# Retention and top-2 experts in one kernel: x turned on TensorE, expert 0's slots from a one-hot of their own, the state in 64x64 blocks

## Chip, cores, metric

One core of one Trainium2 chip runs the whole program. The metric is device time in microseconds, the median of several executions.

## What is computed

The reference is a retention layer (linear attention with decay) whose output goes into a layer of eight experts, two of which serve each token:

```
for t in range(S):
    state = gamma[None, :, None, None] * state + np.einsum('bhd,bhe->bhde', k[:, :, t], v[:, :, t])
    y[:, :, t] = scale * np.einsum('bhd,bhde->bhe', q[:, :, t], state)
...
logits = x @ w_gate
noise_scale = np.log1p(np.exp(x @ w_noise))
noisy_logits = logits + noise_scale * noise
top2 = np.argpartition(-noisy_logits, 2, axis=1)[:, :2]
...
        h = np.maximum(x[mask] @ w1[e], 0.0)
        out[mask] += top2_w[mask, k, None] * (h @ w2[e])
```

There are 4 sequences of 768 tokens, 8 heads of 64, so x has 3072 rows of 512; each expert has 1024 hidden columns. All inputs are f32. top2_w are the two weights after a softmax over the two.

## The kernel before

**Retention loop** (lines 629 to 656). The sequences are cut into chunks of 128 tokens, 6 to a sequence (b), 24 in all (j). `qk(j)` makes k times q for the 8 heads (two heads share the array, each in 64 of its rows), and DVE multiplies the result by a mask (`am`). `y_mm(j)` adds the earlier state (q times U, for all but a sequence's first chunk) and am times v in the PSUM tile pY, then updates the state pU by four products of 128 columns of k with 128 of v, two heads at once, of which only the two diagonal 64x64 blocks are wanted (not in a sequence's last chunk). ACT copies those blocks to U and takes the sum of squares of pY. `x_scale` makes a power of two of it on DVE. `x_split` has ACT scale pY into f32 (`xs`) and copy that to an f16 high part, GpSimd subtract it to get an f16 low part, and SP issue two DMAs: a transpose of both parts into `xt` and a write to `xbuf` in HBM. Three chunks later `logits` multiplies xt by the gate weights.

**Routing** of a sequence is done by DVE while the next sequence runs in the loop: `route_a` to `route_c` (logits, noise, top two, their one-hots `oh` and `mb`), `route_d` (the slot of each token and choice among the 56 blocks of 128 slots, 7 to an expert), `route_e` for each of the two choices: a one-hot of the slot's lane (`a`, 6 x 128 columns), one of its block (`ob`, 6 x 56), and `bb`, ob times five numbers of the token (two for its index, three for its gate; 6 x 5 x 56 = 1680 columns). `route_f` multiplies a by bb on PE and adds the product to a table `acc`, from which `slots` takes the token and the gate of every slot, and `rows_of` the row indices `idx`. The dictionary `todo` says in which chunk each step is issued.

**Experts.** `gather` fetches rows of xbuf by idx (GpSimd), `x_t` transposes them by DMA into XE, `mm1` makes 8 units of hidden columns (12 matmuls each, then ACT `hh` and DVE `hl`, the f16 high and low parts), `mm2` one block of 128 output rows (24 matmuls), and `put` adds it to `out` in HBM. Weights are split into f16 high and low parts too (`w_load`, `w_sum`, `w_hi` on ACT, `w_lo` on DVE or `w_lo_pool` on ACT and GpSimd). The first 384 slots of expert 0 are known once two sequences are routed. Behind the loop the 11 units of these 384 slots (8 mm1, 3 mm2) are spread by `early` between the last sequence's routing; then come expert 0's columns from 384 on, the other experts in the order of their load (`ranks`), and a loop for what overflows.

The order on every engine is that in which the program issues instructions (`manual_schedule`); each engine runs its own in that order, and DMAs of SP are issued in order too. PSUM has 8 banks: pA three, pY two, pU, pR and pL one each.

## Time and profile before

| | us |
|---|---|
| median of 3 runs | 730.25 (729.0 to 732.25) |
| profiled execution, span from first to last instruction | 727.5 |
| PE busy in it | 678.9 |
| DVE / ACT / POOL busy | 290.4 / 311.2 / 235.6 |

The three runs give the time; of the profiled execution the span is the time that is known, and it is 2.75 us under the median. PE is TensorE, PEld its loading of weights, DVE VectorE, ACT ScalarE, POOL GpSimd, SP the engine that issues most DMAs. Busy shares say little by themselves, since the retention loop and the experts have different limits; the views by stretch of time tell them apart.

### The profile page before, as it was taken

What the parts mean: (1) busy time and instruction counts of PE and PEld (TensorE: products, weight loads), DVE (VectorE), ACT (ScalarE), POOL (GpSimd) and SP (SyncE); (2) the same over time, 40 slices, a digit from 0 to 9 for tenths busy, and PEclk for the clock granted to TensorE, in tenths of its full rate; (3) what the DMA queues carried; (4) which work ended last, traced back from release to release, by engine and by line L of the source; (5) the groups of instructions that cost most, each with busy time, mean ns of one, the idle gap of its engine ahead of it and who ended that gap; (6) DMA issues with size and microseconds to landing.
All of it is one profiled execution on the core that took longest, in us unless ns stands there. A gap on an engine that the chain in (4) does not pass through costs nothing.

```text
span 727.5 us, 12014 instructions
## 1 busy us (share of the span) xinstructions
PE 678.9 (93%) x4789; PEld 428.2 (59%) x4789; DVE 290.4 (40%) x719; ACT 311.2 (43%) x562; POOL 235.6 (32%) x186
## 2 busy tenths in 40 slices
PE   8998797967989999999999999999999999999991
PEld 6898696965558555465545545554555466446540
DVE  4338669656852762215222421522152234215100
ACT  4655363435214554435444534444344445344110
POOL 4665553542243320441144024304311421240021
PEclk9999796757999999999999999999999999999996
DMA  9999898775658963668367636745673685453132
GB/s 334 239 330 324 276 281 243 220 162 194 226 119 235 232 184 108 115 110 271 40 117 124 240 53 123 195 133 95 119 237 67 118 193 167 71 104 59 14 44 30
DMA packets 116057, 119.09 MB, mean 164 GB/s; under 512 B 82560, under 2 KB 82816, under 8 KB 112416
## 3 DMA queue, kind: packets, MB, share of 16 engines
q1 hardware_dynamic: 104080, 91.25, 45.1%
q0 software_dynamic: 11344, 26.22, 19.5%
q8 instruction: 38, 0.62, 0.4%
q10 hardware_dynamic: 576, 0.84, 0.3%
q14 instruction: 19, 0.16, 0.1%
HBM read 72.67 MB, written 26.21 MB: 136 GB/s over the span
## 4 chain that ended last, share of the span: by engine, by line
PE 65%; DMA 11%; DVE 10%; issue 6%; ACT 3%; POOL 2%; SPq 0%; POOLq 0%; ACTq 0%; DVEq 0%
PE pH L672 10%; PE pH L674 10%; PE pH L673 10%; PE pO L702 8%; PE pO L703 8%; PE pO L704 8%; DMA out<-ot,idx 6%; PE pY L320 2%; DVE am L309 2%; DVE bb L478 2%; DMA xe<-xg 2%; PE pY L316 2%; PE pU L324 1%; DMA xg<-xbuf,idx 1%; PE pA L306 1%
## 5 line engine op out<-in xcount | busy, mean ns | idle before, releaser
L693 POOL DMA_INDIRECT out<-ot,idx x54 | 85.6, 1586 | 350.8 <-ACT ot L688 210.5
L672 PE MATMUL pH<-xe,w1h 128*128 128x384 f16 (+4 forms) x544 | 176.0, 324 | 1.5 <-DMA xe<-xg 1.5
L674 PE MATMUL pH<-xe,w1l 128*128 128x384 f16 (+4 forms) x544 | 176.0, 323 | 0.0
L673 PE MATMUL pH<-xe,w1h 128*128 128x384 f16 (+4 forms) x544 | 176.0, 323 | 0.0
L676 DVE SCALAR_TENSOR_TENSOR hl<-pH,hh 128x384 f16<-128x384 f32 (+4 forms) x136 | 74.6, 549 | 207.9 <-ACT hh L675 207.7
L704 PE MATMUL pO<-w2h,hl 128*128 128x512 f16 x384 | 145.5, 379 | 0.3 <-DVE hl L676 0.3
L703 PE MATMUL pO<-w2l,hh 128*128 128x512 f16 x384 | 145.5, 379 | 0.0
L702 PE MATMUL pO<-w2h,hh 128*128 128x512 f16 x384 | 145.5, 379 | 0.0
L675 ACT ACTIVATE hh<-pH 128x384 f16<-128x384 f32 (+4 forms) x136 | 65.7, 483 | 133.5 <-PE pH L674 133.5
L688 ACT ACTIVATE ot<-pO,gse 128x512 f32<-128x512 f32 (+4 forms) x54 | 37.0, 686 | 174.0 <-PE pO L704 169.5
L197 DVE SCALAR_TENSOR_TENSOR w1l<-wst,wsc,w1h 128x1024 f16<-128x1024 f32 x32 | 41.8, 1312 | 106.8 <-ACT w1h L192 106.8
L673 PEld LDWEIGHTS <-w1h 128*128 128x128 f16 x544 | 53.3, 98 | 34.4 <-issue 2.2
L674 PEld LDWEIGHTS <-w1l 128*128 128x128 f16 x544 | 53.3, 98 | 34.3 <-issue 0.3
L672 PEld LDWEIGHTS <-w1h 128*128 128x128 f16 x544 | 53.9, 99 | 32.7 <-issue 0.3
L175 ACT ACTIVATE junk<-wst 128x1024 bf16<-128x1024 f32 x64 | 67.2, 1049 | 3.5 <-DMA wst<-w 3.2
L591 POOL DMA_INDIRECT xg<-xbuf,idx x54 | 56.9, 1054 | 27.1 <-issue 15.4
L704 PEld LDWEIGHTS <-hl 128*128 128x128 f16 x384 | 37.5, 98 | 46.0 <-DVE hl L676 0.8
L702 PEld LDWEIGHTS <-hh 128*128 128x128 f16 x384 | 38.1, 99 | 44.1
L703 PEld LDWEIGHTS <-hh 128*128 128x128 f16 x384 | 37.5, 98 | 44.2
L320 PE MATMUL pY<-vp,am 128*128 128x64 f32 x384 | 60.6, 293 | 0.0
L320 PEld LDWEIGHTS pY<-vp,am 128*128 128x128 f32 x384 | 58.4, 221 | 0.6 <-issue 0.2
L344 POOL TENSOR_TENSOR x<-xs,x 128x512 f16<-128x512 f32 x23 | 29.2, 1269 | 54.8 <-ACT x L343 26.4
(163 smaller groups left out, 767.2 us busy)
## 6 DMA issues: line engine op xcount, KB each, us to landing
wst<-w SPq DMA_DIRECT2D x28, 1024.0 KB, 7.5
in_q<-qT SPq DMA_DIRECT2D x24, 256.0 KB, 4.6
in_k<-kT SPq DMA_DIRECT2D x24, 256.0 KB, 4.7
in_v<-vt SPq DMA_DIRECT2D x24, 256.0 KB, 4.9
in_kt<-kt SPq DMA_DIRECT2D x24, 256.0 KB, 5.0
xbuf<-x SPq DMA_DIRECT2D x24, 256.0 KB, 3.7
...
```

The costliest lines, as they stand in the source:

```text
L175: nc.scalar.activation(junk, st[:, i * 1024:(i + 1) * 1024], AF.Square, accum_out=ss[:, i:i + 1])
L320: nc.tensor.matmul(pY[:, 2 * i + s, :], AM[j][:, s, i, :], VP[j][:, 2 * i + s, :], start=(not c and i == 0 and s == 0), stop=True, skip_gr ...
L591: nc.gpsimd.indirect_dma_start(out=x[:n], out_offset=None, in_=xbuf[:128 + B0 * S] if e == 0 and t < 3 else xbuf, in_offset=bass.IndirectO ...
L672: nc.tensor.matmul(p[:, :n], whi, xh, start=(k == 0), stop=False)
L673: nc.tensor.matmul(p[:, :n], whi, xl, start=False, stop=False)
L674: nc.tensor.matmul(p[:, :n], wlo, xh, start=False, stop=(k == KT - 1))
L675: nc.scalar.activation(hh[:, f, n0:n1], p[:, :n], AF.Relu)
L676: nc.vector.scalar_tensor_tensor(hl[:, f, n0:n1], p[:, :n], 0.0, hh[:, f, n0:n1], op0=OP.max, op1=OP.subtract)
L693: nc.gpsimd.indirect_dma_start(out=out, out_offset=bass.IndirectOffsetOnAxis(ap=idx[:n, i:i + 1], axis=0), in_=ot[:n], in_offset=None, com ...
L702: nc.tensor.matmul(p, a, WT["2h"][:, f, :], start=(f == 0), stop=False)
L703: nc.tensor.matmul(p, a, WT["2l"][:, f, :], start=False, stop=False)
L704: nc.tensor.matmul(p, c, WT["2h"][:, f, :], start=False, stop=(f == FT - 1))
```

## The change

- **x on TensorE.** x_split makes the f16 high part straight from pY on ACT and the low part on DVE; the DMA transpose and GpSimd's subtraction go. `x_turn` of chunk j - 2 does eight f16 transposes on PE into a new PSUM tile pX (one bank), and ACT copies it to xt. pA has two banks in place of three; mm1 uses pA, pA and pX in turn. logits stands ahead of y_mm and has 12 matmuls of 16 columns in place of 8 of 32 and 16.
- **Routing.** Expert 0's slots have a one-hot of their own over its 7 blocks (`own_a`, `own_b`, `own_c`), in the loop. The other 49 blocks (`rest_c`, `rest_d` on DVE, `rest_e` on PE; 294 and 1470 columns) are made after the loop, in eight parts, four of them ahead of expert 0's columns from 384 on and four between its units; their table is in PSUM (BIGT) until the eleventh unit, then `ranked` sorts it.
- **State.** pU is made by eight products of 64 columns of k with 64 of v, one a head; each writes 64 partitions.
- **Times of other work.** Expert 0's weights are loaded and split some 4 to 9 chunks earlier, the zeros of out are written in chunks 12 to 18, not after the loop, and `early` lets one unit through between smaller steps.

SP's queue around one chunk in the loop before, seven rows (in_q, in_k, in_v and in_kt are the four inputs of a chunk, wst weights, x and xt the two parts of x and their transpose):

```order
L221 DMA in_q<-qT 128x512
L221 DMA in_k<-kT 128x512
L221 DMA in_v<-vt 128x512
L221 DMA in_kt<-kt 128x512
L171 DMA wst_582<-w 128x1024
L346 DMA_TRANSPOSE xt<-x_609 128x8x128
L347 DMA xbuf<-x_609 128x1024
```

and around the thirteenth chunk now (out<-zero is one write of 1 MB):

```order
L353 DMA xbuf<-x_1192 128x1024
L228 DMA in_q<-qT 128x512
L228 DMA in_k<-kT 128x512
L228 DMA in_v<-vt 128x512
L228 DMA in_kt<-kt 128x512
L253 DMA out<-zero 512x1x512
L353 DMA xbuf<-x_1275 128x1024
```

The transposes have left SP's queue, and in some chunks a write of zeros stands there.

DVE in the loop before, where a sequence's route_e stands (L468 to L478) ahead of the next chunk's mask product:

```order
L457 CAST lf<-lb 128x24
L468 TENSOR_TENSOR ob<-blks,lf 128x336
L470 TENSOR_TENSOR a<-lanes,lf 128x768
L478 TENSOR_TENSOR bb<-ob,vv 128x1680
L309 TENSOR_TENSOR am<-pA,ct 128x512 x2
L152 TENSOR_SCALAR p2m<-xss 128x1
L153 TENSOR_SCALAR xsc<-p2m 128x1
```

and now, from the lane one-hot of own_a (L474) over the next chunk's low part of x, mask product and x_scale to own_b:

```order
L474 TENSOR_TENSOR a<-lanes,lf_1269 128x768
L352 SCALAR_TENSOR_TENSOR x_1275<-pY,xsc,x_1275 128x512
L317 TENSOR_TENSOR am<-pA,ct 128x512 x2
L159 TENSOR_SCALAR p2m<-xss 128x1
L160 TENSOR_SCALAR xsc<-p2m 128x1
L162 TENSOR_SCALAR invx<-p2m 128x1
L482 CAST tokb<-gateb 128x6
L483 TENSOR_TENSOR gr<-gateb,tokb 128x6
L484 CAST tokb<-gr 128x6
L485 TENSOR_TENSOR tokb<-gr,tokb 128x6
L495 TENSOR_TENSOR ob_1358<-blks,lf_1269 128x42
L499 TENSOR_TENSOR bb_1360<-ob_1358,tokb 128x210
```

The one-hots of 336 and 1680 columns are gone from here; narrow ones of 42 and 210 are in their place, a chunk later than the lane's, and the low part of x (L352) is new.

DVE where expert 0's columns from 384 on begin, before (L676 is hl of one unit):

```order
L532 TENSOR_REDUCE capd<-cm 128x7
L680 TENSOR_TENSOR i_2484<-wsc_584,wsc_1221 128x1
L683 TENSOR_SCALAR gse<-wacc,i_2484 128x4
L676 SCALAR_TENSOR_TENSOR hl<-pH,hh 128x256 x8
L676 SCALAR_TENSOR_TENSOR hl<-pH,hh 128x192 x8
```

and now (L758 is hl, L541 to L551 one part of rest_c and rest_d):

```order
L485 TENSOR_TENSOR vvb<-gr,vvb 128x12
L758 SCALAR_TENSOR_TENSOR hl<-pH,hh 128x256
L541 TENSOR_TENSOR ob<-blks,lfa 128x294
L543 TENSOR_TENSOR a<-lanes,lfa 128x768
L551 TENSOR_TENSOR bb<-ob,vvb 128x1470
L758 SCALAR_TENSOR_TENSOR hl<-pH,hh 128x256 x2
L541 TENSOR_TENSOR ob<-blks,lfa 128x294
L543 TENSOR_TENSOR a<-lanes,lfa 128x768
L551 TENSOR_TENSOR bb<-ob,vvb 128x1470
```

Between the units' hl there now stand the wide one-hots of the other experts.

The diff, cut to its core:

```diff
-    pU = psum.tile([128, HP, 128], F32, name="pU")
+    pU = psum.tile([128, 512], F32, name="pU")[:, :HP * 64].rearrange("p (a d) -> p a d", a=HP)
...
-        pA = [psum.tile([128, HP, C], F32, name="pA", bufs=3) for _ in range(2)]
+        pA = [psum.tile([128, HP, C], F32, name="pA", bufs=2) for _ in range(2)]
...
         if c < NC - 1:
             for i in range(HP):
-                nc.tensor.matmul(pU[:, i, :], IN["kt", j][:, i * 128:(i + 1) * 128],
-                                 VP[j][:, 2 * i:2 * i + 2, :].rearrange("p h d -> p (h d)"),
-                                 start=(c == 0 and i == 0), stop=True, skip_group_check=True)
+                for s in range(2):
+                    h = 2 * i + s
+                    nc.tensor.matmul(pU[s * 64:s * 64 + 64, i, :], IN["kt", j][:, h * 64:h * 64 + 64], VP[j][:, h, :],
+                                     start=(c == 0 and i == 0), stop=True, skip_group_check=True)
...
-                nc.scalar.activation(un[r, :, r], pU[r, :, r], AF.Copy)
+                nc.scalar.activation(un[r, :, r], pU[r], AF.Copy)
...
-    def x_split(j, eng=None):
-        xs = work.tile([128, DM], F32, name="xs", bufs=2)
-        x = work.tile([128, 2, DM], F16, name="x16", bufs=2)
-        nc.scalar.activation(xs, PY.pop(j), AF.Copy, scale=XS[j])
-        nc.scalar.activation(x[:, 0], xs, AF.Copy)
-        (eng or nc.gpsimd).tensor_tensor(x[:, 1], xs, x[:, 0], op=OP.subtract)
-        XT[j] = work.tile([128, 2 * KT, C], F16, name="xt", bufs=4)
-        nc.sync.dma_start_transpose(XT[j], x.rearrange("p a d -> p (a d)"))
+    def x_split(j):
+        x = X16[j] = work.tile([128, 2, DM], F16, name="x16", bufs=3)
+        py = PY.pop(j)
+        nc.scalar.activation(x[:, 0], py, AF.Copy, scale=XS[j])
+        nc.vector.scalar_tensor_tensor(x[:, 1], py, XS[j], x[:, 0], op0=OP.mult, op1=OP.subtract)
         nc.sync.dma_start(xbuf[128 + j * C:128 + (j + 1) * C, :], x.rearrange("p a d -> p (a d)"))
+
+    def x_turn(j):
+        x = X16.pop(j)
+        p = psum.tile([128, 2 * KT, C], F16, name="pX")
+        for a in range(2):
+            for i in range(KT):
+                nc.tensor.transpose(p[:, a * KT + i, :], x[:, a, i * 128:(i + 1) * 128], identh)
+        XT[j] = work.tile([128, 2 * KT, C], F16, name="xt", bufs=2)
+        nc.scalar.activation(XT[j], p, AF.Copy)
...
+        x = XT.pop(j)
         for i in range(KT):
-            nc.tensor.matmul(PL[:, c].rearrange("p s e -> p (s e)"), XT[j][:, i, :],
-                             wg2[:, v, i].rearrange("p s e -> p (s e)"), start=(i == 0), stop=False,
-                             skip_group_check=True)
-            nc.tensor.matmul(PL[:, c, 0, :], XT[j][:, KT + i, :], wg2[:, v, i, 0, :], start=False, stop=(i == KT - 1),
-                             skip_group_check=True)
+            for n, (a, w) in enumerate(((i, 0), (i, 1), (KT + i, 0))):
+                nc.tensor.matmul(PL[:, c], x[:, a, :], wg2[:, v, i, w], start=(i == 0 and n == 0),
+                                 stop=(i == KT - 1 and n == 2), skip_group_check=True)
...
+        a = work.tile([128, NC, 128], BF, name="a", bufs=3)
+        nc.vector.tensor_tensor(a, lanes[:, None, :].to_broadcast([128, NC, 128]),
+                                lf[:, 0, :, None].to_broadcast([128, NC, 128]), op=OP.is_equal)
+        R["own", b] = (lf, a)
...
+        ob = work.tile([128, NC, NBLK], BF, name="ob0")
...
+        nc.vector.tensor_tensor(ob, blks[:, None, :NBLK].to_broadcast(s3), lf[:, 1, :, None].to_broadcast(s3),
+                                op=OP.is_equal)
+        bb = work.tile([128, NC, NV, NBLK], BF, name="bb0")
...
+        nc.vector.tensor_tensor(bb, ob[:, :, None, :].to_broadcast(s4), tokb[:, sl, :, None].to_broadcast(s4), op=OP.mult)
+        R["own", b] = (a, bb)
+
+    def own_c(b):
+        a, bb = R.pop(("own", b))
+        for c in range(NC):
+            nc.tensor.matmul(LST, a[:, c, :], bb[:, c], start=(c == 0), stop=(c == NC - 1), skip_group_check=True)
...
+    def rest_c(b, k):
+
+        lf, vv = lfa[:, b], vvb[:, b]
+        a = work.tile([128, NC, 128], BF, name="a", bufs=3)
+        bb = work.tile([128, NC, NV, NCB], BF, name="bb", bufs=3)
+        ob = work.tile([128, NC, NCB], BF, name="ob", bufs=1)
+        s3 = [128, NC, NCB]
+        nc.vector.tensor_tensor(ob, blks[:, None, NBLK:].to_broadcast(s3), lf[:, 1, k, :, None].to_broadcast(s3),
                                 op=OP.is_equal)
-        nc.vector.tensor_tensor(a[:, k], lanes[:, None, :].to_broadcast([128, NC, 128]),
+        nc.vector.tensor_tensor(a, lanes[:, None, :].to_broadcast([128, NC, 128]),
                                 lf[:, 0, k, :, None].to_broadcast([128, NC, 128]), op=OP.is_equal)
-
...
-            if n:
-                s4 = [128, NC, n, NCOL]
-                eng.tensor_tensor(bb[:, k, :, v], ob[:, k, :, None, :].to_broadcast(s4),
-                                  vv[:, k, :, v, None].to_broadcast(s4), op=OP.mult)
...
+        R["rest", b, k] = (a, bb, ob)
+
+    def rest_d(b, k):
+
+        a, bb, ob = R["rest", b, k]
+        s4 = [128, NC, NV, NCB]
+        nc.vector.tensor_tensor(bb, ob[:, :, None, :].to_broadcast(s4),
+                                vvb[:, b, k, :, :, None].to_broadcast(s4), op=OP.mult)
+
+    def rest_e(b, k):
+        a, bb, ob = R.pop(("rest", b, k))
+        for c in range(NC):
+            nc.tensor.matmul(BIGT, a[:, c, :], bb[:, c], start=(b == 0 and k == 0 and c == 0),
+                             stop=(b == B - 1 and k == 1 and c == NC - 1), skip_group_check=True)
...
-    steps = (route_a, route_b, route_c, route_h, route_d, route_e, route_e, route_f, route_g)
...
+        j = (b + 1) * NC
+        last = b == B - 2
+        for n, f in zip((2, 3, 3, 3, 4, 5, 5, 6, 7, 7) if not last else (2, 2, 3, 3, 4, 4, 4, 5, 5, 5),
+                        (route_a, route_b, route_m, route_c, route_n, route_d, rest_a, own_a, own_b, rest_b)):
+            at(j + n, f, b)
+        late[j + 3] = lambda b=b: route_p(b)
+        if not last:
+            late[j + 7] = lambda b=b: own_c(b)
...
     for i in range(4):
-        at(5 + 2 * i, w_load, 0, "1", i)
-        at(7 + 2 * i, w_sum, 0, "1", i)
-        at((14, 15, 17, 18)[i], w_hi, 0, "1", i)
-        at((15, 16, 18, 19)[i], w_lo, 0, "1", i)
-        at(13 + 2 * i, w_load, 0, "2", i)
-        at((15, 17, 19, 21)[i], w_sum, 0, "2", i)
+        at((1, 2, 3, 4)[i], w_load, 0, "1", i)
+        at((4, 5, 6, 7)[i], w_sum, 0, "1", i)
+        at((8, 9, 10, 11)[i], w_hi, 0, "1", i)
+        at((8, 9, 10, 11)[i], w_lo, 0, "1", i)
+        at((7, 8, 9, 10)[i], w_load, 0, "2", i)
+        at((12, 13, 14, 15)[i], w_sum, 0, "2", i)
+        at((16, 17, 18, 19)[i], w_hi, 0, "2", i)
+        at((17, 18, 19, 20)[i], w_lo_pool, 0, "2", i)
...
+    todo[8].insert(0, (w_scale, (0, "1")))
+    todo[16].insert(0, (w_scale, (0, "2")))
...
+    for i in range(7):
+        at(12 + i, zero_out, i)
...
+        if j >= 3:
+            logits(j - 3)
...
-            x_split(j - 1)
...
-        y_mm(j)
-        if j >= 3:
-            logits(j - 3)
...
         for f, a in todo.get(j, []):
             f(*a)
+        if j:
+            x_split(j - 1)
+        if j >= 2:
+            x_turn(j - 2)
+        y_mm(j)
+        if j in late:
+            late[j]()
...
-        p = psum.tile([128, 512], F32, name="pH", tag="pA", bufs=3)
+        MM[0] += 1
+        p = psum.tile([128, 512], F32, name="pH", **(dict(tag="pX") if MM[0] % 3 == 0 else dict(tag="pA", bufs=2)))
...
+    BIGT = psum.tile([128, 512], F32, name="pB", tag="pU")[:, :NV * NCB].rearrange("p (v n) -> p v n", v=NV)
+    j = NCH - 1
+    x_scale(j)
     early(1)
-    route_f(b - 1)
-    logits(NCH - 3)
-    w_lo_pool(0, "2", 2)
+    x_turn(j - 1)
+    x_split(j)
+    parts = [(b, k) for b in range(B) for k in range(2)]
+
+    done = []
+
+    def rest(n):
+        while done:
+            rest_e(*done.pop(0))
+        for _ in range(n):
+            if parts:
+                p = parts.pop(0)
+                done.append(p)
+                rest_c(*p)
+                rest_d(*p)
+
     early(1)
-    logits(NCH - 2)
-    w_lo_pool(0, "2", 3)
+    own_c(b - 1)
+    rest(1)
+    logits(j - 2)
+    x_turn(j)
+    logits(j - 1)
     early(1)
-    logits(NCH - 1)
+    logits(j)
     route_a(b)
+    early(1)
     route_b(b)
     out_scale(0, 0, 3)
-    early(3)
+    route_m(b)
+    early(1)
     route_c(b)
-    route_h(b)
+    early(1)
+    route_p(b)
+    route_n(b)
+    early(1)
     route_d(b)
-    route_e(b, 0)
-    early(3)
-    route_e(b, 1)
-    for i in range(7):
-        zero_out(i)
-    route_f(b)
+    own_a(b)
+    early(1)
+    own_b(b)
+    early(1)
+    own_c(b)
     slots(3, NBLK)
     for t in range(3, NBLK):
         gather(0, t)
         x_t(0, t)
-    early(len(units))
-    slots(NBLK, NCOL)
+    rest_a(b)
     ranks()
-    out_scale(0, 3, NBLK)
-    for t in range(3):
-        put(0, t, first[t])
     for r in range(E - 1):
         order.append(nc.sync.value_load(eid[0:1, r:r + 1], min_val=1, max_val=E - 1))
     w_load(1, "1", 0, 2)
     w_load(1, "1", 2, 2)
+    out_scale(0, 3, NBLK)
+    for n in (2, 1):
+        early(1)
+        rest(n)
+    early(len(units))
+    rest_b(b)
+    for t in range(3):
+        put(0, t, first[t])
...
+                if e == 0 and n in (0, 2, 5, 8):
+                    rest(1)
+                if e == 0 and n == 10:
+                    rest(0)
+                    slots(NBLK, NCOL)
+                    ranked()
...
             if e == 0 and n == 2:
-                route_g(b - 1)
-                route_g(b)
+                rank_caps()
                 loop_table()
```

## Rows read from the trace of the kernel before

**Rows 1.** The page: its first line, and of the span in 40 equal slices the clock that was granted to TensorE.

```profile
span 727.5 us, 12014 instructions
...
PEclk9999796757999999999999999999999999999996
```

**Rows 2.** Busy time by stretch, 20 and 100 us long: us in the stretch, then busy us (and instructions) of PE, PEld, DVE, ACT and POOL, granted clock, DMA share, GB/s.

```profile
600.00:700.00 100.00, 100.00 (x543) 52.98 (x542) 29.34 (x48) 37.07 (x61) 22.62 (x16) 1.00 0.39 79
```

**Rows 3.** The timeline in the retention loop: start, us, engine, line, operation, tiles, shapes, count, and in brackets idle time before and what ended it. PEld is the loading of weights. L306 is qk, L320 the product with v in y_mm, L324 the state update; the last row is the last group of the last chunk's y_mm.

```profile
9.61 0.97 PEld L306 LDWEIGHTS pA<-qs,in_k 64*128 64x128 f32 x16 [1.85 <-POOL qs L286]
...
10.70 1.86 PEld L320 LDWEIGHTS pY<-vp,am 128*128 128x128 f32 x16
...
12.54 1.11 PE L324 MATMUL pU<-vp,in_kt 128*128 128x128 f32 x8
...
13.58 1.16 PE L306 MATMUL pA<-qs,in_k 64*128 64x128 f32 x16
...
43.52 1.16 PE L306 MATMUL pA<-qs,in_k 64*128 64x128 f32 x16 [0.20 <-POOL qs L286]
...
48.57 1.16 PE L306 MATMUL pA<-qs,in_k 64*128 64x128 f32 x16
...
167.06 0.95 PE L320 MATMUL pY<-vp,am 128*128 128x64 f32 x4
```

**Rows 4.** Busy time by stretch of 7 us, columns as in rows 2.

```profile
41.00:48.00 7.00, 6.80 (x73) 6.57 (x73) 2.42 (x9) 3.98 (x8) 4.80 (x5) 1.00 1.14 311
...
76.00:83.00 7.00, 2.48 (x20) 2.10 (x21) 6.96 (x9) 2.65 (x6) 2.22 (x2) 0.81 0.95 342
83.00:90.00 7.00, 7.00 (x41) 6.76 (x41) 1.64 (x6) 1.91 (x4) 5.03 (x5) 0.50 0.67 178
```

**Rows 5.** The timeline of DVE around 75 us: the first block of route_e (L468 ob, L470 a, L478 bb) and the mask product am behind it.

```profile
73.50 1.30 DVE L468 TENSOR_TENSOR ob<-blks,lf 128x336 bf16<-128x336 bf16 x1
74.72 0.94 DVE L470 TENSOR_TENSOR a<-lanes,lf 128x768 bf16<-128x768 bf16 x1
75.59 2.97 DVE L478 TENSOR_TENSOR bb<-ob,vv 128x1680 bf16<-128x1680 bf16 x1
78.48 1.28 DVE L309 TENSOR_TENSOR am<-pA,ct 128x512 f32<-128x512 f32 x2
```

**Rows 6.** Busy time by stretch, columns as in rows 2: most of the first half of the retention loop, and a stretch in which six zero writes of 1 MB run.

```profile
20.00:76.00 56.00, 50.86 (x567) 48.68 (x565) 30.68 (x106) 31.13 (x72) 34.46 (x31) 1.00 1.11 310
...
174.00:188.00 14.00, 11.35 (x85) 7.09 (x86) 8.87 (x35) 6.07 (x11) 5.12 (x2) 0.88 1.01 367
```

**Rows 7.** Small matmuls: the timeline of PE with two of the logits' matmuls, the first two of expert 0's columns 384 to 640, and the four transposes of a tail block (L726), merged in one row; then L726 by itself, with the shortest, median and longest of its 24 in ns.

```profile
180.77 0.17 PE L356 MATMUL pL<-wg,xt 128*128 128x16 f16 x1
180.79 0.18 PE L353 MATMUL pL<-wg,xt 128*128 128x32 f16 x1
...
213.16 0.27 PE L672 MATMUL pH<-xe,w1h 128*128 128x256 f16 x1 [0.16 <-DMA xe<-xg]
213.27 0.27 PE L673 MATMUL pH<-xe,w1h 128*128 128x256 f16 x1
...
252.15 0.60 PE L726 MATMUL pO<-ct,yt 128*64 128x128 f32 x4
...
L726 PE MATMUL pO<-ct,yt x24: 272/272/273, 252.1 to 588.8; 128*64 128x128 f32 x8, 128*32 128x128 f32 x8, 128*48 128x128 f32 x4, 128*16 128x128 f32 x4
```

**Rows 8.** Groups by line and shape from 20 to 160 us: line, engine, operation, tiles, shapes, count | busy us, mean ns of one | idle time before.

```profile
L309 DVE TENSOR_TENSOR am<-pA,ct 128x512 f32<-128x512 f32 x42 | 26.9, 681 | 18.4 <-PE pA L306 18.4
L344 POOL TENSOR_TENSOR x<-xs,x 128x512 f16<-128x512 f32 x21 | 26.9, 1280 | 39.6 <-issue 14.4 <-ACT x L343 11.2 <-DMA wst<-w 6.4
...
L343 ACT ACTIVATE x<-xs 128x512 f16<-128x512 f32 x21 | 13.2, 630 | 0.9 <-DMA xbuf<-x 0.3
...
L392 DVE TENSOR_TENSOR oh<-ct,i 128x54 f32<-128x54 f32 x6 | 7.0, 1198 | 0.1
...
L197 DVE SCALAR_TENSOR_TENSOR w1l<-wst,wsc,w1h 128x1024 f16<-128x1024 f32 x4 | 6.0, 1504 | 0.0
...
L153 DVE TENSOR_SCALAR xsc<-p2m 128x1 int32<-128x1 int32 x21 | 3.2, 154 | 0.7
```

**Rows 9.** The same view from 160 to 216 us.

```profile
L192 ACT ACTIVATE w2h<-wst,wsc 128x1024 f16<-128x1024 f32 x4 | 4.2, 1133 | 0.0
...
L676 DVE SCALAR_TENSOR_TENSOR hl<-pH,hh 128x256 f16<-128x256 f32 x1 | 0.4, 425 | 5.3 <-ACT hh L675 5.3
...
L392 DVE TENSOR_TENSOR oh<-ct,i 128x54 f32<-128x54 f32 x2 | 0.3, 211 | 0.0
```

**Rows 10.** The timeline between the retention loop and the rest of expert 0: of DVE two rows of route_e and idx, the row indices of the blocks from column 384 on; of PE the last routing product (L485) and the first two matmuls of an mm2 (L702, L703).

```profile
164.65 1.90 DVE L478 TENSOR_TENSOR bb<-ob,vv 128x1680 bf16<-128x1680 bf16 x1
...
193.63 0.51 DVE L468 TENSOR_TENSOR ob<-blks,lf 128x336 bf16<-128x336 bf16 x1
...
203.62 0.17 DVE L506 SCALAR_TENSOR_TENSOR idx<-tk,padv 128x4 int32<-128x4 f32 x1
...
201.76 0.89 PE L485 MATMUL pR<-bb,a 128*128 128x280 bf16 x6 [2.23 <-DVE bb L478]
202.48 0.38 PE L702 MATMUL pO<-w2h,hh 128*128 128x512 f16 x1
202.70 0.38 PE L703 MATMUL pO<-w2l,hh 128*128 128x512 f16 x1
```

More of the change, by code (lines that the diff above doesn't have):

```diff
@@ L423, in route_c @@
[L423 to L433 removed]
+        R[b] = (oh, cb, t2)
+    def route_d(b):
+        oh, cb, t2 = R[b]
+        sl = slice(b * NC, (b + 1) * NC)
+        nc.vector.tensor_tensor(posb[:, sl], POS[:, :NC, :], t2, op=OP.add)
+        cn = work.tile([128, NL], F32, name="cum")
+        nc.vector.tensor_tensor(cn, POS[:, NC, :], R["cum"], op=OP.add)
+        if b == B0 - 1:
+            nc.vector.tensor_scalar(cn[:, E:NL], cn[:, 0:1], float(FIRST), None, op0=OP.max)
+        R["cum"] = cn
@@ new lines, in gate_parts, with own_b @@
+    def gate_parts(dst, g, shape):
+        n = int(np.prod(shape))
+        r = work.tile([128, 2 * NC], F32, name="gr")[:, :n].rearrange("p (k c) -> p k c", c=NC)
+        nc.vector.tensor_copy(dst[2], g)
+        nc.vector.tensor_tensor(r, g, dst[2], op=OP.subtract)
+        nc.vector.tensor_copy(dst[3], r)
+        nc.vector.tensor_tensor(dst[4], r, dst[3], op=OP.subtract)
+    def own_b(b):
+        l = E if b >= B0 else 0
+        sl = slice(b * NC, (b + 1) * NC)
+        lf, a = R["own", b]
+        gate_parts([tokb[:, None, sl, v] for v in range(NV)], gateb[:, None, sl, l], [1, NC])
+        ob = work.tile([128, NC, NBLK], BF, name="ob0")
+        s3 = [128, NC, NBLK]
+        nc.vector.tensor_tensor(ob, blks[:, None, :NBLK].to_broadcast(s3), lf[:, 1, :, None].to_broadcast(s3),
+                                op=OP.is_equal)
+        bb = work.tile([128, NC, NV, NBLK], BF, name="bb0")
+        s4 = [128, NC, NV, NBLK]
+        nc.vector.tensor_tensor(bb, ob[:, :, None, :].to_broadcast(s4), tokb[:, sl, :, None].to_broadcast(s4), op=OP.mult)
+        R["own", b] = (a, bb)
@@ L455, in route_d @@
         nc.vector.tensor_scalar(lb[:, 1], si, 7, None, op0=OP.arith_shift_right)
[L456 to L468 removed]
+        nc.vector.tensor_copy(lfa[:, b], lb)
@@ L471, in route_e @@
                                 lf[:, 0, k, :, None].to_broadcast([128, NC, 128]), op=OP.is_equal)
-        m = 3 if b == B - 1 else NV
-        for eng, v in ((nc.vector, slice(0, m)), (nc.gpsimd, slice(m, NV))):
-            n = v.stop - v.start
-            if n:
-                s4 = [128, NC, n, NCOL]
-                eng.tensor_tensor(bb[:, k, :, v], ob[:, k, :, None, :].to_broadcast(s4),
-                                  vv[:, k, :, v, None].to_broadcast(s4), op=OP.mult)
-    def route_f(b):
-        oh, g, ps, lf, vv, a, bb, ob = R[b]
-        for k in range(2):
-            for c in range(NC):
-                nc.tensor.matmul(LST, a[:, k, c, :], bb[:, k, c], start=(k == 0 and c == 0),
-                                 stop=(k == 1 and c == NC - 1), skip_group_check=True)
-        if b == 0:
-            nc.vector.tensor_copy(acc, LST)
-        else:
-            nc.vector.tensor_tensor(acc, acc, LST, op=OP.add)
+        R["rest", b, k] = (a, bb, ob)
@@ L523, in ranks, with ranked @@
         nc.vector.tensor_copy(eid, rk)
+        R["pm"] = pm, cm
+    def ranked():
+        m = E - 1
+        s3, s4 = [128, m, m], [128, m, NBLK, m]
+        pm, cm = R["pm"]
         tp = wp = hp.tile(s4, F32, name="tp")
@@ L645, in moe_kernel @@
             load(j + AHEAD)
-        y_mm(j)
-        if j >= 3:
-            logits(j - 3)
-        if j == NCH - 1:
-            todo[j] = [(x_scale, (j,)), (x_split, (j, nc.vector)), (w_hi, (0, "2", 0)), (w_lo, (0, "2", 0))] + todo[j]
-            for i in range(1, 4):
-                at(j, w_hi, 0, "2", i)
-                if i < 2:
-                    at(j, w_lo, 0, "2", i)
         for f, a in todo.get(j, []):
             f(*a)
+        if j:
[5 more added lines that the diff above has]
+            late[j]()
     lctx.close()
```

151 lines of the change are left out of this document (76 added, 75 removed).

## The prediction

> **What bounds the kernel now.** I read the page first, then the engines by stretch, then PE's timeline of the retention loop, then DVE where PE stops. The page gives a span of 727.5 us and a PEclk row that falls below 9, but for the tail, only in its fifth to tenth slice of 18 us, between some 73 and 182 us [rows 1]. From 213 us PE never stops: in 600 to 700 it is busy for 100.00 of 100 us at clock 1.00 [rows 2]. So the experts are bound by PE, and a microsecond taken off before 213 us is worth a microsecond at the end, as long as nothing starves PE later.
>
> The retention loop runs to about 167.5 us, where the last y_mm ends [rows 3]. Its full-speed price is the distance of two qk groups with no wait: 5.05 us (43.52 to 48.57), and 3.97 for the chunk that begins a sequence (9.61 to 13.58); the chunk that ends one lacks pU and is taken alike. Sixteen of the one and eight of the other, less one qk at the end, are 112 us; the loop takes 158 (9.6 to 167.5) [rows 3]. **Some 46 us are lost in it.** The windows show where: 41 to 48 is full and at 1.00, 76 to 83 has PE busy 2.48 of 7 with DVE at 6.96, and the stretch behind it runs at 0.50 [rows 4]. DVE's rows for the first place are the one-hots of routing: ob 1.30, a 0.94, bb 2.97, with the mask product am, which PE waits for, queued behind them at 78.48 [rows 5]. That block (route_e) comes six times before 177 us. First the wait, then the half clock (1.2 GHz) behind it: both have one cause, a long block on DVE.
>
> **Transposes move to PE.** Removed: 24 DMA transposes. They cost no wait of their own size: with them the DMA engines were busy 1.11 of their time at 310 GB/s over 20 to 76 us, and PE still kept within some 0.4 us a chunk of its full-speed price; 367 GB/s ran where big plain transfers ran [rows 6]. New w1/w2 loads come earlier and 6.3 MB of zeros are written during chunks 12 to 18. Up to in_q of chunk 22 some 39 MB must land by about 110 us, 355 GB/s, under 367 but close; I charge 5 us for DMA over the loop, 0 to 10.
>
> Added on PE, each chunk: eight f16 transposes of 128 columns. A 256-column f16 matmul starts 0.11 us after the one before (213.16, 213.27), so 128 columns take about 0.055, 0.45 for eight [rows 7]. Upper bound: the four f32 transposes of the tail take 0.60, 0.11 apart, so 0.9. The logits become twelve matmuls for eight; they start 0.02 to 0.03 apart [rows 7], +0.1. Together +0.55 a chunk, 13 us in 24 chunks (10 to 24). Nothing excludes more, see the rivals.
>
> Added on ACT: the copy of pX, 1024 elements; w_hi has that size and takes 1.13; the second copy x, 0.63, goes [rows 8, 9]. ACT gets to about 3.4 us a chunk, 5.6 where w_hi and w_lo_pool's scaling join it (chunks 17 to 19), still about PE's period: nothing, if U is copied on time, which has 1.9 us of cover (qk, logits, transposes). On POOL the subtraction, 1.28, goes; on DVE it comes back from PSUM, as am, 0.68 [rows 8].
>
> **64x64 state blocks.** Four matmuls of 128x128 become eight of 64x64; the four take 1.11 now [rows 3]. Bounds: eight 64-column y products with full 128x128 weights load them in 1.86, so at worst +0.9; the eight qk products, each on one half of the array's rows, load theirs in 0.97 for 128 columns [rows 3], so with half the columns perhaps 0.5, which is -0.5. I take -0.2, near the qk row, because these blocks too are halves: 20 chunks, -4 us (-10 to +18). qk already changes from the whole array to halves and back: its loads end at 10.58 and the y loads begin at 10.70, 0.12 later [rows 3]. The Trainium skill, TensorEngine Tiling (Array Packing), Tiling Modes, Key Properties, says that a change of the tiling mode drains the engine, which speaks against this edit; one more change in 20 chunks at that row's 0.12 would make the sum 2.4 us longer.
>
> **Routing.** The wide one-hots leave the loop: six blocks of ob, a, bb. In place comes a narrow one (7 columns of blocks): a 0.94 and small rows. DVE a chunk then: two am 1.36, pow2 three rows of 0.15, x low part 0.68 less overlap, 2.4 in all [rows 8], plus about 15 us of routing per sequence, 29 per six chunks against PE's 31. The sum fits, the peaks don't: the chunk with max, indices and one-hots (oh took 1.20 each in the loop [rows 8] and 0.21 behind it, with POOL still [rows 9]) has about 6.8 on DVE, where 5.6 fit before x_turn or pY makes PE wait. The second sequence has four w_lo of 1.5 on top [rows 8]. I charge 5.5 us of waits and 3 for half clock behind them.
>
> **Loop, sum.** 9.6 + 112 + 13 - 4 + 5 + 5.5 + 3 = 144, against 167.5: **23 us gained**.
>
> **From the last y_mm to the first matmul on columns 384 up** it takes 45.6 us now (213.16). In this stretch PE has eight mm1 units (12 matmuls, 0.164 each, from 0.11 x 384/256) and three mm2 (24 by 0.22 [rows 10]): 31 us; the rest is small work and waits, for the last three route_e blocks above all. In the new order I followed PE and DVE side by side. DVE: x_lo, a first rest part, route_a to route_m with hl between, own slots, all done near 25; idx, then what the trace shows from idx (203.62) over gather and transposes to 213.16, 9.5 us [rows 7, 10]: ready at 35. PE: 31 + three rest_e + transposes, logits, some 37, and 1.7 of waits for pX, which x_turn and every third mm1 share. So 38.5: **7 us gained** (1 to 10).
>
> **Expert 0 pays.** rest_c and rest_d, eight parts, are not hidden by the loop any more. A part is ob 0.46 (0.51 for 336 columns, now 294), a 0.87, bb 1470 elements, 1.67 (1.90 for 1680): 3.0 us of DVE [rows 10]. Four are issued ahead of column 384: part 0 in the routing chain, inside the 38.5, three under mm2, which asks nothing of DVE. The rest are queued between the hl of columns 384 up, 0.43 each [rows 9], with PE's rest_e of the same part close behind: at unit 2 PE comes about 1.3 us early, at unit 10 about 1.2, and the ranked table (2.6) then holds hl for 1.5. Three pH buffers cover the others. 4 us of waits, 3.2 us for five rest_e (six matmuls, 0.72 with 280 columns, now 245 [rows 10]): **7 us lost** (4 to 15). Expert 1's gathers come 20 us before its first matmul, as now.
>
> **Sum.** 144 + 38.5 + (727.5 - 213.2) + 7.2 = 704.2 us of span. The median shown, 730.25, is 2.75 above the profiled span; with the same 2.75: 707.
>
> **Rivals.**
> 1. *DVE still sets the loop.* For it: oh and ob grew while POOL worked, oh near six times [rows 5, 8, 9]; against: POOL's load falls by a third. If every sequence costs 35 us of DVE, the loop ends near 158: 721. Chance 0.18.
> 2. *rest blocks PE in expert 0.* By the rows above DVE and PE each have some 53 us of work between the loop's end and ranked. If the parts run as slowly as bb's 2.97 [rows 5], 10 us more: 717. Chance 0.08.
> 3. *The loop is not shortened*: PE takes back in added work what it no longer waits, by the upper bounds of pU and transposes (+18, +11) less the smaller waits. Loop end near 167, the other terms cancel: 730. Chance 0.06.
> 4. *Slower: the transposes are not pipelined.* One f32 transpose takes 0.272 from its start to its end [rows 7]. If each of the eight is paid at that, in every chunk before y_mm, 2.2 us in place of 0.45, +42 us: 749. It decides from 1.4 us per eight, where the 23 us are eaten. Against it: the four rows overlap, 0.60 for four. Chance 0.04. TensorE: Matmul & The Clock Gate of the Trainium skill (Part 4, PE-mode transpose) gives 275 to 390 ns for one 128x128 bf16 transpose; by that the time would be near 750 as an estimate, and the overlap of these four speaks against it.
>
> **How the numbers follow.** The forecast has 0.64, with a range of its own of 694 to 718: pU's gain (-6 more), fewer waits (-7), against waits twice as long. With rival 2 and most of rival 1 it is 0.85 up to 726; I give 694 to 726. This kernel's runs can tell 0.5%, so 726.6 and 733.9 are the bounds of "the same": rivals 1 and 2 and the forecast are faster, 0.89 after a small part of 1 is taken off, rival 3 the same, 0.06, rival 4 slower, 0.05 with a chance left for what I have not seen.
>
> **What would show it.** qk groups 5.2 to 5.8 us apart through the whole loop, PEclk at 9 in the slices where it fell, the last y_mm near 144 (right), near 158 with DVE full (rival 1). Eight transposes in about 0.5, eight pU blocks in at most 1.1. The first 384-up matmul some 38 us behind the last y_mm. In expert 0 waits of PE on bb, 4 us in all. DMA's queue above 350 GB/s with POOL's qs waiting for in_q near chunk 18 would say that zeros cost more. Wrong is the whole reading if DVE is idle and PE busy, yet the loop ends behind 160: then the added PE work is what I sized wrongly.

## The result, and the profile after

The changed kernel takes 707.65 us (median of 4 runs, 706.82 to 711.02), the kernel before 731.25 in the same job: ratio 0.968, 95% interval 0.9645 to 0.9714. The prediction was 707. A second job, with a second trace of the same kernel, gave 0.9706 (0.9639 to 0.9772). Ratios are taken from undisturbed runs alone, while the times given are medians of all runs, and of the ninth kernel below only the ratio is used, since its profile fell into a disturbed run.

The page of the changed kernel, first trace (this execution took 711.02 us), beside [rows 1]:

```profile
span 709.2 us, 12929 instructions
...
PEclk8799899799999999999999999999999999999996
```

The clock row falls in fewer slices than before, though not in none. PE's timeline of the retention loop, for [rows 3] (each f32 product stands as two records); the last two rows are the last y_mm and the first matmul on columns 384 up:

```profile
28.56 0.69 PE L334 MATMUL pU<-vp,in_kt 128*64 128x64 f32 x16
29.17 1.16 PE L314 MATMUL pA<-qs,in_k 64*128 64x128 f32 x16
30.27 0.46 PE L370 MATMUL pL<-wg,xt 128*128 128x16 f16 x12
30.58 0.61 PE L360 MATMUL pX<-identh,x 128*128 128x128 f16 x8
31.02 0.44 PE L324 MATMUL pY<-U,qs 128*128 128x128 f32 x2
...
34.41 1.16 PE L314 MATMUL pA<-qs,in_k 64*128 64x128 f32 x16
...
150.43 0.56 PE L328 MATMUL pY<-vp,am 128*128 128x64 f32 x4
...
189.04 0.27 PE L754 MATMUL pH<-xe,w1h 128*128 128x256 f16 x1
```

The distance of two qk groups is 5.24 us (29.17 to 34.41). The eight 64x64 products reach the next qk in 0.61, where the four 128x128 needed 1.04 [rows 3]; the twelve logits take 0.31 and the eight transposes 0.44 to the next group (30.58 to 31.02). What PE waited for from 9 to 150 us, in the first trace (engine, line waited for: us in total, times, longest):

```profile
PE pL L370 <- ACT xt L362: 2.8, 2, 1.4
PE pR L505 <- DVE bb L499: 2.7, 1, 2.7
PE pX L360 <- DVE x L352: 1.8, 3, 0.8
PE pA L314 <- POOL qs L293: 1.4, 1, 1.4
```

7.3 us inside the loop (the last row lies ahead of it). And the same from 189 to 216 us, in expert 0 (the last row is PE behind ranked):

```profile
PE pB L557 <- DVE bb L551: 1.5, 2, 1.0
PE pH L754 <- DVE hl L758: 1.4, 1, 1.4
```

The two traces have the same waits in the loop (7.3 us) and differ in the clock. Windows of 7 us (columns as in [rows 2]) of the first trace:

```profile
12.00:19.00 7.00, 7.00 (x52) 6.54 (x51) 2.07 (x10) 2.84 (x9) 3.38 (x3) 0.50 1.05 387
19.00:26.00 7.00, 7.00 (x59) 6.60 (x59) 1.67 (x3) 3.21 (x10) 2.27 (x2) 0.56 1.04 390
68.00:75.00 7.00, 6.47 (x56) 6.18 (x52) 5.67 (x19) 3.64 (x6) 0.00 (x0) 0.61 0.72 245
131.00:138.00 7.00, 7.00 (x67) 6.54 (x67) 4.74 (x13) 3.16 (x7) 5.86 (x5) 0.51 0.32 89
```

and of the second (span 702.4, this execution took 704.2):

```profile
12.00:19.00 7.00, 7.00 (x97) 6.61 (x96) 3.25 (x12) 4.38 (x13) 4.11 (x4) 1.00 1.05 386
19.00:26.00 7.00, 7.00 (x99) 6.62 (x97) 4.22 (x14) 5.11 (x13) 3.84 (x4) 1.00 1.05 399
...
117.00:124.00 7.00, 7.00 (x55) 6.78 (x56) 5.82 (x24) 3.01 (x5) 1.55 (x1) 0.50 0.29 108
124.00:131.00 7.00, 7.00 (x73) 6.54 (x73) 4.16 (x23) 1.45 (x4) 5.98 (x6) 0.61 0.48 133
```

PE is busy 7.00 of 7 at 12 to 19 us in both, with 52 instructions at clock 0.50 and 97 at 1.00. The loop ends at 151.0 in the first and at 142.6 in the second; from there to column 384 it is 38.05 in both. The second trace's last y_mm and first matmul on columns 384 up:

```profile
142.05 0.56 PE L328 MATMUL pY<-vp,am 128*128 128x64 f32 x4
...
180.66 0.27 PE L754 MATMUL pH<-xe,w1h 128*128 128x256 f16 x1
```

### The profile page after: what moved, and what is told of

It is laid out like the page before. It is cut to its first block, busy times and chain, and to the rows that moved or that the text cites. A ratio compares the mean times of both kernels' runs of the same rounds, so it can differ in the third digit from the quotient of the medians.

```text
span 709.2 us, 12929 instructions
## 1 busy us (share of the span) xinstructions
PE 677.8 (96%) x5261; PEld 427.9 (60%) x5261; DVE 298.6 (42%) x773; ACT 320.3 (45%) x564; POOL 208.2 (29%) x163
## 4 chain that ended last, share of the span: by engine, by line
PE 86%; DVE 8%; DMA 2%; issue 1%; ACT 1%; POOL 0%; SPq 0%; POOLq 0%; ACTq 0%
PE pH L754 12%; PE pH L756 12%; PE pH L755 12%; PE pO L784 11%; PE pO L785 11%; PE pO L786 11%; PE pY L328 5%; PE pA L314 3%; PE pY L324 3%; PE pU L334 2%; PE pX L360 1%; DVE bb L551 1%; PE pL L370 1%; DVE am L317 1%; PE pT L798 1%
## 5 line engine op out<-in xcount | busy, mean ns | idle before, releaser
L775 POOL DMA_INDIRECT out<-ot,idx x54 | 87.8, 1625 | 353.4 <-ACT ot L770 205.6
L758 DVE SCALAR_TENSOR_TENSOR hl<-pH,hh 128x384 f16<-128x384 f32 (+4 forms) x136 | 74.3, 549 | 194.0 <-ACT hh L757 193.8
L328 PE MATMUL pY<-vp,am 128*128 128x64 f32 x384 | 58.0, 284 | 0.0
L328 PEld LDWEIGHTS pY<-vp,am 128*128 128x128 f32 x384 | 55.6, 212 | 0.1
L287 POOL TENSOR_TENSOR vp<-in_v,ct 128x512 f32<-128x512 f32 x24 | 26.6, 1109 | 68.0 <-issue 48.7
```

The lines of the kernel that those rows point to most:

```text
L328: nc.tensor.matmul(pY[:, 2 * i + s, :], AM[j][:, s, i, :], VP[j][:, 2 * i + s, :], start=(not c and i == 0 and s == 0), stop=True, skip_gr ...
L758: nc.vector.scalar_tensor_tensor(hl[:, f, n0:n1], p[:, :n], 0.0, hh[:, f, n0:n1], op0=OP.max, op1=OP.subtract)
L775: nc.gpsimd.indirect_dma_start(out=out, out_offset=bass.IndirectOffsetOnAxis(ap=idx[:n, i:i + 1], axis=0), in_=ot[:n], in_offset=None, com ...
```

## The experiments

**Theory A**: the loop was held by the wide one-hots on DVE, and taking them out gained most. **Theory B**: it was held by the transposes on the DMA engines.

**1. Transposes by DMA again** (of the change, this part undone).

```diff
+        XT[j] = work.tile([128, 2 * KT, C], F16, name="xt", bufs=4)
+        nc.sync.dma_start_transpose(XT[j], x.rearrange("p a d -> p (a d)"))
...
-                nc.tensor.transpose(p[:, a * KT + i, :], x[:, a, i * 128:(i + 1) * 128], identh)
...
```

> The changed kernel with one part undone: x is transposed by DMA again (24 transposes on SP's queue, no pX, no copy to xt); routing, 64x64 state, weights and zeros stay as changed. Theory A (the wide one-hots on DVE set the old loop; the transposes by themselves bought little): PE saves 0.6 us a chunk, some 14 us, and pays waits for transfers, so 697 to 712 against 707.7 with them. Theory B (the transposes by DMA held the old loop back, and taking them off the queues is what gained): 718 or more, with POOL's qs waiting for in_q in most chunks and the DMA engines moving near 310 GB/s in place of 390 to 400.

724.97 us against 727.39 for before: ratio 0.9969 (0.9926 to 1.0012). The whole gain is gone, as B said. One of B's signs is missing: POOL waited only once for in_q (0.4 us); PE waited for xt itself. The first of its waits from 9 to 167 us, and its window that answers to 19 to 26 above:

```profile
PE pL L366 <- DMA xt<-x: 12.0, 6, 2.4
```

```profile
19.00:26.00 7.00, 4.90 (x64) 4.45 (x63) 4.22 (x14) 4.57 (x13) 3.93 (x4) 1.00 1.16 307
26.00:33.00 7.00, 7.00 (x68) 6.64 (x68) 0.75 (x1) 1.86 (x6) 1.69 (x2) 0.64 1.14 308
```

The DMA engines are full at 307 GB/s, where 399 move in the second trace, with the transposes on PE; PE waits for xt, and then runs at 0.64.

**2. State in 128x128 blocks again.**

```diff
-                    nc.tensor.matmul(pU[s * 64:s * 64 + 64, i, :], IN["kt", j][:, h * 64:h * 64 + 64], VP[j][:, h, :],
...
+                nc.tensor.matmul(pU[:, i, :], IN["kt", j][:, i * 128:(i + 1) * 128],
...
```

> The changed kernel with one part undone: the state product is four matmuls of 128x128 again in place of eight of 64x64. From the traces, the group takes 0.61 us to the next qk group in the changed kernel and 0.97 to 1.04 in the one before, so 20 groups cost 7 to 9 us more: 714 to 717. A rival says that the time is hidden by DVE's am (DVE sets the loop still): under 710.

702.74, ratio 0.9663 (0.9591 to 0.9735): no slower than the change, where 714 to 717 was expected. Its qk groups are 5.57 apart (23.79 to 29.36), 0.33 more than with 64x64, yet its loop ends at 143.6, 1.0 behind the second trace of the change. Two of them:

```profile
23.79 1.16 PE L314 MATMUL pA<-qs,in_k 64*128 64x128 f32 x16
...
29.36 1.16 PE L314 MATMUL pA<-qs,in_k 64*128 64x128 f32 x16
```

It waits only 0.3 us on bb where the change waits 2.7, and loses 3.4 us at half clock where the second trace loses 6.9 (counted as in the table of the loop further below).

**3. Both undone: routing and the timetable of weights and zeros alone.**

> The changed kernel with two parts undone, transposes by DMA and four 128x128 state products: what stays is the routing (own slots of expert 0 in the loop, the rest behind it) with the new timetable of weights and zeros. Theory A (routing is what gained): the time of the kernel with DMA transposes alone plus 7 to 9, 705 to 720. Theory B (transposes by DMA held the loop): 725 or more, near the 731 of the kernel before.

722.92, ratio 0.9919 (0.9879 to 0.9959). By the median 0.8% of the 3.2% is left. The time lies between the two forecasts (705 to 720 and 725 or more): A's hung on the first run's time and failed with it, B's is missed by 2 us.

**4. Four wide parts made a second time in the loop.**

```diff
+            for k in range(2):
+                at(j + 8 + k, rest_c, b, k)
+                at(j + 8 + k, rest_d, b, k)
```

> The changed kernel plus four wide parts (ob 294 columns, a, bb 1470 columns; 3.1 us of DVE each) made a second time inside the loop, in chunks 14, 15, 20 and 21, and thrown away; all else as changed. Theory A (such a block on DVE costs PE the wait and the half clock behind it): 2 to 4.5 us each, 716 to 726. If DVE has room for a block in a chunk, as its busy share of 4.6 of 7 us in the loop says: under 710.

726.48, ratio 0.997 (0.9924 to 1.0016): 0.029 above the change, some 21 us, over 5 for each block of 3.1, more than the 2 to 4.5 expected. A's mechanism holds as well. Its waits from 9 to 168 us, and one of the added rows:

```profile
PE pL L370 <- ACT xt L362: 7.1, 4, 2.6
PE pR L424 <- DVE mb L412: 5.2, 2, 3.4
PE pX L360 <- DVE x L352: 4.2, 3, 2.4
```

```profile
145.37 3.00 DVE L541 TENSOR_TENSOR ob<-blks,lfa 128x294 bf16<-128x294 bf16 x1
```

16.5 us of waits for 7.3, and 25.7 us lost at half clock behind them. That ob takes 0.46 elsewhere; here POOL's vp (1.05) and qs (1.27) ran beside it.

So both loads count. **Theory D**: either one alone keeps PE waiting, so that the gain needs both parts. The next four runs were on one chip (before: 731.68).

**5. The change itself again.**

> The changed kernel itself, on the same chip as the three others, with a second trace. Its ratio to the kernel before should be 0.968 again (0.964 to 0.972). If the half clock between 12 and 26 us of its first trace belongs to the kernel, the second trace shows it at the same place; if it is chance, the loop ends 4 to 6 us earlier, at 144 to 147, and this run is faster by as much. Against the run with 128x128 state products (ratio 0.966) it tells whether the 64x64 blocks gain anything.

709.72, ratio 0.9706 (0.9639 to 0.9772), runs from 704.2 to 712.45. The early fall of the clock was absent from this trace; its loop ended 8.4 us earlier.

**6. w2's low parts on DVE alone.**

```diff
-        at((17, 18, 19, 20)[i], w_lo_pool, 0, "2", i)
+        at((17, 18, 19, 20)[i], w_lo, 0, "2", i)
```

> The changed kernel with one helper exchanged: the low parts of w2 in chunks 17 to 20 are made by DVE (one row of 1.28 us each) and no more by ACT's scaled copy (1.14) and POOL's subtraction (2.13). Theory C: while POOL's subtraction runs, DVE's rows between SBUF tiles are stretched (gr 1.97 in place of 0.17, ov 1.71 for 0.22, ob 1.07 for 0.20, bb 1.36 for 0.38, some 6.6 us in all), and that makes the 2.7 us wait of PE on bb and the half clock behind it: 4 to 9 us faster than the changed kernel. Rival: DVE is simply full in these chunks, and 5.1 us of rows more than eat what the stretching cost: the same within 2, or slower.

705.26, ratio 0.9625 (0.956 to 0.9689), 4.5 us under the fifth run by the medians, though the two intervals overlap. The traces are clearer. POOL and DVE of the change, first trace, chunk 19:

```profile
120.89 2.14 POOL L212 TENSOR_TENSOR w2l<-wst,w2h 128x1024 f16<-128x1024 f32 x1
```

```profile
121.08 1.97 DVE L483 TENSOR_TENSOR gr<-gateb,tokb 128x6 f32<-128x6 f32 x1
...
123.39 1.07 DVE L495 TENSOR_TENSOR ob<-blks,lf 128x42 bf16<-128x42 bf16 x1
...
124.49 1.36 DVE L499 TENSOR_TENSOR bb<-ob,tokb 128x210 bf16<-128x210 bf16 x1
```

The same rows of the sixth run:

```profile
120.49 0.17 DVE L483 TENSOR_TENSOR gr<-gateb,tokb 128x6 f32<-128x6 f32 x1
...
120.98 0.20 DVE L495 TENSOR_TENSOR ob<-blks,lf 128x42 bf16<-128x42 bf16 x1
121.21 0.38 DVE L499 TENSOR_TENSOR bb<-ob,tokb 128x210 bf16<-128x210 bf16 x1
```

A subtraction of six numbers a lane (gr) takes 1.97 us beside POOL's 2.14, and 0.17 without it. The slow ob and bb stand beside POOL's next steps, vp (123.35, 1.04) and qs (124.35, 1.26), not beside the subtraction itself. PE's wait on bb (2.7) is gone, the clock stays at 1.00 from 117 to 131, and the loop ends at 146.5 where the first trace, with the same early half clock, ends at 151.0. Theory C holds for the rows and the wait; of ob and bb it named the wrong neighbour.

**7. The kernel before with the transposes on PE alone** (pX, x_turn, two pA buffers; nothing else).

> The kernel before with one part of the change alone: x is transposed on TensorE (pX, copy to xt by ACT, two pA buffers in place of three), routing with its wide one-hots, 128x128 state, weights and zeros as before. Theory B (transposes by DMA held the old loop, whatever the routing): 12 us faster than before or more. Theory D (each of the two loads, the transposes on the DMA engines and the wide blocks on DVE, alone keeps PE waiting, so that the gain needs both parts): within 6 us of before.

742.78, ratio 1.0157 (1.0088 to 1.0226): 11 us slower. B, which forecast 12 us or more faster, falls as a cause by itself; D's forecast (within 6 us of before) is missed too. The added work on PE is not the whole of it: PE now also waits for the copy to xt and for POOL's low part x. One wait of the kernel before has shrunk, though, that on qs, which POOL makes from in_q. PE and POOL in the loop before:

```profile
PE pA L306 <- POOL qs L286: 8.0, 8, 2.1
```

```profile
POOL qs L286 <- DMA in_q<-qT: 14.9, 11, 2.5
```

and PE in run 7:

```profile
PE pX L354 <- ACT xt L356: 6.2, 7, 1.4
...
PE pA L308 <- POOL qs L287: 2.7, 2, 1.4
PE pX L354 <- POOL x L346: 2.7, 2, 1.4
```

POOL there waits for in_q once, 0.4 us, and the DMA engines are busy 0.79 of their time from 20 to 76 us, for 1.11 before [rows 6]. So a part of PE's waits in the kernel before goes with the transposes by DMA; how much is theirs is not settled, since POOL in run 7 also stands longer at x, ahead of qs, waiting for ACT (51.6 us for 12.9). The four corners, as ratios to before (run 7 differs from the change in more than the row says: its low part is made on POOL, its state products are 128x128 and its logits stand behind y_mm):

| | transposes by DMA | transposes on PE |
|---|---|---|
| routing, weights, zeros as before | 1 | 1.016 (run 7) |
| as changed | 0.997 (run 1) | 0.968, 0.971 |

**8. As run 1, with the zeros behind the loop again.**

```diff
-    for i in range(7):
-        at(12 + i, zero_out, i)
...
+    for i in range(7):
+        zero_out(i)
```

> The changed kernel with transposes by DMA, as in the first run, and the 6.3 MB of zeros written behind the loop again. If the transposes cost by the rate that they leave to the transfers (the first run moved 307 to 340 GB/s where the changed kernel moves 385 to 405), 6.3 MB less are 15 to 20 us less of transfers within the loop: 8 us or more faster than the first run (725). If they cost by their own latency (logits wait for xt, 12.0 us in the first run, in PE's queue ahead of y_mm), the zeros matter little: within 4 us of the first run.

724.03, ratio 0.9889 (0.9797 to 0.998). By the ratios some 6 us of run 1's loss are the zeros, but the intervals overlap: undecided between the two. The traces say more: from 80 to 137 us, where run 1 writes the zeros, PE waits 5.8 us on xt in run 1 and 0.9 here. Up to 167 us PE still waits 7.1 us on xt, with the DMA engines full at mostly 290 to 310 GB/s.

**9. As run 8, with the logits behind y_mm, where they were before.**

```diff
-        if j >= 3:
-            logits(j - 3)
         ...
         y_mm(j)
+        if j >= 3:
+            logits(j - 3)
```

> The changed kernel with transposes by DMA and the zeros behind the loop, as in the run at 0.989 of before, and the logits of chunk j-3 put behind y_mm of chunk j again, with route_a behind them, as in the kernel before. If it is the place of the logits ahead of y_mm that makes the transposes by DMA expensive (7.1 us of waits on xt in that run, and the half clock behind them), this one is 8 us faster or more, ratio 0.978 or less. If the transposes cost through the rate of transfers wherever the logits stand, the waits move to qs and am and the ratio stays at 0.985 to 0.995.

Ratio 0.9883 (0.9825 to 0.9941), as in run 8. The place of the logits in PE's queue isn't the reason. Whether it is the rate of transfers was not tested by itself: the transposes also hold SP's queue, 1.26 us each in run 1 (median) where a load of in_q takes 0.40.

**10. Three losses taken from the change.**

```diff
-WARM, BUSY = 10, 5
+WARM, BUSY = 10, 10
...
-        late[j + 3] = lambda b=b: route_p(b)
+        late[j + 3] = lambda b=b: (route_c(b), route_p(b))
...
-        at((17, 18, 19, 20)[i], w_lo_pool, 0, "2", i)
+        at((17, 18, 19, 20)[i], w_lo, 0, "2", i)
```

> The changed kernel with three of the losses that its traces show taken away: low parts of w2 by DVE (as in the run at 0.9625), ten warm-up matmuls in place of five between the first two qk groups, so that PE idles 0.1 to 0.4 us there in place of 1.1 to 1.5, and the exponential of route_c behind y_mm, so that ACT's copy to xt no longer stands behind a wait for DVE's den (PE waits 1.4 us twice on xt). From the second trace of the changed kernel (loop end 142.6, 704.2): 4 us for the low parts, 3 for xt and the half clock behind it: 694 to 701, ratio 0.950 to 0.960. If DVE's total work sets the loop, only the 4 us come: ratio above 0.960.

697.12 us (695.66 to 697.98), ratio 0.9547 (0.9517 to 0.9576): faster than both kernels, and the spread of the times shrinks to 2.3 us. The clock on its page:

```profile
PEclk9999999999999999999999999999999999999996
```

Nowhere below 9 until the tail. The waits on xt (2.8) and on bb (2.7) are gone, and the loop ends at 133.1. What each of the three gives here was not taken apart.

**11. Run 10 with 128x128 state products.**

> The run before this with four 128x128 state products in place of eight 64x64. In the traces a chunk is 5.57 us with them and 5.24 with 64x64, yet the whole kernel with 128x128 was no slower, because PE waited for DVE in chunks 17 to 19 either way. If that is the reason, it is slower here, where those waits are shorter: by 3 to 7 us. If the 64x64 blocks cost elsewhere what they save, it is the same within 2.

698.5, ratio 0.9572 (0.9537 to 0.9607). Its loop ends at 136.9, 3.8 behind run 10, but the times lie 1.4 apart with overlapping intervals. What 64x64 is worth stays open between nothing and some 5 us.

**12. The longer warm-up alone.**

> The changed kernel with ten warm-up matmuls in place of five between the first two qk groups, nothing else. In its first trace PE idled 1.43 us ahead of the second qk group and ran at 0.50 to 0.56 from 12 to 26 us; in its second it idled 1.14 there and ran at 1.00, and its loop ended 8 us earlier. If that wait is what the clock falls behind, all runs come out like the second trace, 703 to 705 with little spread, ratio 0.962 to 0.966; if the fall has another cause, the runs stay spread over 704 to 712, ratio 0.968 to 0.971.

709.45, ratio 0.9715 (0.9684 to 0.9746). PE idles 0.24 ahead of the second qk group and the early fall is absent from its trace, but the clock falls to 0.73 at 61 to 68 and to 0.50 at 124 to 131, behind the waits on xt and bb, and the time is no better. The first forecast (703 to 705) was wrong: without the early fall, as far as one trace shows, the median is the same. Run 10 also takes away those waits, and holds the clock.

## Why the prediction was right, and where it was not

By its own steps, for the first and the second trace:

| step | predicted | first | second |
|---|---|---|---|
| last y_mm ends | 144 | 151.0 | 142.6 |
| from there to column 384 | 38.5 | 38.05 | 38.05 |
| from there to the end | 521.5 | 520.2 | 521.7 |
| span | 704.2 | 709.2 | 702.4 |

The loop taken apart, from the second qk group to the last y_mm: what PE waited for in it, what the clock cost (windows of 7 us, each times what its granted clock lacks to 1), and the rest, which is PE's work at full speed. A wait in a stretch of half clock is counted twice, so the rest can be a few us low.

| | loop | waits | half clock | rest |
|---|---|---|---|---|
| before | 158.4 | 20.9 | 25.1 | 112.4 |
| run 7: before, transposes on PE | 164.5 | 14.6 | 25.2 | 124.7 |
| run 1: change, transposes by DMA | 156.8 | 17.8 | 33.5 | 105.5 |
| change, first trace | 141.4 | 7.3 | 15.3 | 118.8 |
| change, second trace | 132.9 | 7.3 | 6.9 | 118.7 |
| run 10 | 123.4 | 3.3 | 0.0 | 120.1 |

The prediction's reading of the loop, 112 us of work and 46 lost, is borne out. Its path too: PE does more work and is kept waiting less. That 707 comes within a microsecond of 707.65 is in part luck, since the two executions' loops end 8.4 us apart, and terms off by -5 (DMA), +12.3 or +3.9 (half clock), -2.6 (state) and +1.8 (waits) cancel in part.

- **Transposes on PE**: right in size. Eight reach the next group in 0.44 (predicted 0.45). Run 2, whose state products are those of before, has 5.57 a chunk for 5.05: transposes and logits take 0.52, for a predicted 0.55. Rival 4 (2.2 a chunk) is out.
- **Transposes off the DMA queues**: here the prediction was wrong in its reading, not in its sum. It said that they cost no wait of their own size. Against that stand the 8.0 us on qs in the kernel before, which are 2.7 in run 7. That the waits "have one cause, a long block on DVE" was too narrow as well: of the 20.9 us of waits in the loop before, am and cum, DVE's, are 9.1. In the changed program the transposes by DMA would cost 0.029 of 727, some 21 us (run 1), most of it through the clock: PE has 13 us less work there, but waits 10.5 longer and loses 33.5 at half clock, for 15.3 or 6.9. The sum was safe, since it priced the program without them: for its 5 us for DMA (0 to 10) nothing was measured, as no wait of PE on a transfer stands among the four above, at 382 to 406 GB/s in full windows; the bound of 367 came from too slow a stretch [rows 6].
- **64x64 blocks**: -0.33 a chunk between run 2 and the second trace, for -0.2; eight products and the change to qk's tiles take 0.61 together, so a price for changing the tiling mode isn't visible. The time showed none of the gain here: the second trace waits 2.4 us longer on bb in chunk 19 and loses 3.5 more at half clock than run 2.
- **Routing**: the waits at DVE's peaks were predicted at 5.5 and measured 7.3, in part elsewhere. 2.8 came through ACT: the exponential of route_c waits there for DVE's den, with the copy to xt behind it. 2.7 came from w_lo_pool, whose effect on DVE the sum left out, though the grown rows of before (oh 1.20 for 0.21, bb 2.97 for 1.90) had the same look [rows 5, 8 to 10].
- **Half clock**: the mis-sized term. Predicted 3; measured 15.3 in the first trace and 6.9 in the second. Part of the 15.3 is the early fall at 12 to 26 us, which stands ahead of all routing and which the prediction didn't have. The rest agrees: 118.8 and 118.7 of full-speed work for a predicted 112 + 13 - 4 = 121.
- **Transition and expert 0**: 38.05 for 38.5. Waits of 2.9 and five rest_e of 0.65, together 6.2, for 7.2; ranked held hl for 1.4 (predicted 1.5).

What the loop gained has two conditions: without the wide blocks on DVE (run 4) and without the transposes on the DMA engines (runs 1, 3, 8 and 9); with the wide blocks back, or with the transposes and the zeros back, nearly all of the 23 us is gone; with the transposes back and the zeros behind the loop some 13 to 15 us are (runs 8 and 9). With the old routing the transposes on PE lose 11. Whether the transposes by DMA collide with the earlier weights or with the denser new order was not settled: no run had the new routing with the old timetable of weights. The first wait on xt in runs 1 and 8 (2.1 and 2.4 us at 26) does fall among the loads of w1, issued there from 17 to 36 us and before from 45 on.
